# q and k of the later head pairs transposed by DMA and reordered by GpSimd, with paced loads and the mask term on ScalarE

## The chip, the cores and the metric

One core of one Trainium2 chip. The metric is the device time of one launch in microseconds (us), with smaller being better. TensorE is called PE below, VectorE DVE, ScalarE ACT, GpSimd POOL; SP is the engine that here only issues DMAs.

## The reference

Attention with four sink columns and a window of 128, then a block that mixes tokens and channels.

```python
# q, k, v: (4, 8, 768, 64); n_sink 4; window 128
scores = scale * q @ k.T
keep = (column < n_sink) | ((row - column >= 0) & (row - column < window))
a = softmax(where(keep, scores, -1e9))
x = (a @ v)  ->  (4, 768, 512), heads side by side

theta = x @ w_theta
zr, zi = x * cos(theta), x * sin(theta)
u = x + w_tok_r @ zr + w_tok_i @ zi          # over tokens
out = u + maximum(u @ w_ch, 0)
```

## The kernel before

The 32 heads are worked in 16 **pairs**, pair i in **slot** i. Slots 4 to 7 belong to batch entry 1, 8 to 11 to entry 2, 12 to 15 to entry 3; behind each four there is a theta stage (`thp`, cosine and sine `cs`, products `zz`). While a slot computes scores, PE fills its gaps with the token mixing (`yp`) and channel mixing (`wp`) of the batch entry before. PE, ACT, POOL and SP take instructions in program order. DVE's order is fixed when the kernel is built, by a scheduler that works with modelled times.

q and k must be transposed. Pairs 0 to 11 are loaded so that partition p holds rows 6p to 6p+5 (long runs in memory), cast to bf16 by POOL, transposed by PE, and put into row order by the copy that evacuates PSUM. Pairs 12 to 15 are loaded in short runs so that the DMA transpose gives the right order at once:

```python
QK_DMA = range(12, NPAIR)

def transposed_by_dma(i):                # called in slot i - 2
    if i not in QK_DMA: return
    for name in ("q", "k"):
        c = qk_c.pop((name, i))
        x = qkt.tile([P, S], BF16, name=f"{name}T", tag=f"{name}T")
        nc.sync.dma_start_transpose(out=x..., in_=c...)
        qk_t[name, i] = x

def transposed(name, i):                 # called in slot i - 1
    if i in QK_DMA: return
    for t in range(NT):                  # 6 blocks of 128 x 128
        nc.tensor.transpose(out=tp[:, t, :], in_=c[:, t, :, :], identity=ident)
    dst, src = x.rearrange("c (p t) -> c p t", t=NT), tp.rearrange("c t p -> c p t")
    ...                                  # nc.scalar.copy, or DVE for pairs 1 to 3
```

In the second half of the mixing the transposes of `u` for token blocks 0 to 2 of entries 1 and 2 go by DMA too, and so do three of four transposes of x (`xT`):

```python
U_PE = {(b, t) for b in range(B) for t in range(NT) if b in (0, B - 1) or t in (3, 4, 5)}
```

The values of the sink columns for entries 2 and 3 are copied from a f32 tile to bf16, times a row mask, four copies each (`vsink<-vsf,rows`). In program order they follow slots 8 and 9:

```python
def sink_values(b):
    for tb in range(NB):
        nc.vector.tensor_scalar(out=vsinks[b % 2][:, tb, :, 0:D], in0=vsf[:, b - 2, :, :],
                                scalar1=rows[:, tb:tb + 1], scalar2=None, op0=ALU.mult)
```

The softmax here doesn't subtract the row's maximum and nothing guards it: scores larger than these inputs give would overflow.

## Time and profile before

| | kernel before |
|---|---|
| time, three runs | 191.49 us (191.43 to 191.65) |
| span in the profile | 189.7 us |
| granted PE clock, mean | 0.998 |
| PE busy | 171.6 us, 90% |
| DVE, ACT, POOL busy | 127.4, 99.6, 70.3 us |

PE is the bound from about 90 us on. To read the timelines: the first two numbers are the start and the length of an instruction (or of x instructions in a row) in us; then the engine, the line of the kernel, the operation, what it writes and reads, the shapes; in brackets the idle time of the engine just before, and what ended it. The theta stage of entry 1 on DVE:

```profile
80.72 1.29 DVE L319 TENSOR_TENSOR zz<-cs,x_nat 128x1024 bf16<-128x1024 bf16 x2 [3.99 <-ACT cs L316]
81.93 0.48 DVE L421 TENSOR_SCALAR vsink<-vsf,rows 128x512 bf16<-128x512 f32 x1
82.64 1.29 DVE L319 TENSOR_TENSOR zz<-cs,x_nat 128x1024 bf16<-128x1024 bf16 x2 [0.23 <-ACT cs L316]
```

Two products take 1.29 us (0.65 each), DVE had been idle for 3.99 before them, and one of the eight sink copies slips in between. Seven come behind. Line numbers are higher in the kernel after: L319 here is L326 there, L421 is L429.

### The profile page before, as it was taken

What the parts mean: (1) busy time and instruction counts of PE and PEld (TensorE: products, weight loads), DVE (VectorE), ACT (ScalarE), POOL (GpSimd) and SP (SyncE); (2) the same over time, 40 slices, a digit from 0 to 9 for tenths busy, and PEclk for the clock granted to TensorE, in tenths of its full rate; (3) what the DMA queues carried; (4) which work ended last, traced back from release to release, by engine and by line L of the source; (5) the groups of instructions that cost most, each with busy time, mean ns of one, the idle gap of its engine ahead of it and who ended that gap; (6) DMA issues with size and microseconds to landing.
All of it is one profiled execution on the core that took longest, in us unless ns stands there. A gap on an engine that the chain in (4) does not pass through costs nothing.

```text
span 189.7 us, 4058 instructions
## 1 busy us (share of the span) xinstructions
PE 171.6 (90%) x1632; PEld 87.8 (46%) x1659; DVE 127.4 (67%) x237; ACT 99.6 (53%) x106; POOL 70.3 (37%) x87
## 2 busy tenths in 40 slices
PE   7776998899998998997999999999999999899972
PEld 2333574554464655443454555434345643344430
DVE  6597676883857788189969673787769726644541
ACT  4575787616973661899965702797462059000000
POOL 8986577858886601314635001670000000000000
PEclk9999999999999999999999999999999999999999
DMA  5999999999999995991239779999623500021121
GB/s 181 318 273 214 321 380 328 371 329 322 340 358 323 299 261 148 236 218 31 83 66 167 167 130 228 217 218 146 153 45 97 152 21 38 30 80 55 59 110 56
DMA packets 65954, 35.88 MB, mean 189 GB/s; under 512 B 54160, under 2 KB 60304, under 8 KB 65936
## 3 DMA queue, kind: packets, MB, share of 16 engines
q1 hardware_dynamic: 64784, 35.59, 74.6%
q0 software_dynamic: 1152, 0.04, 0.6%
q8 instruction: 13, 0.21, 0.5%
q14 instruction: 5, 0.04, 0.1%
HBM read 25.82 MB, written 6.29 MB: 169 GB/s over the span
## 4 chain that ended last, share of the span: by engine, by line
PE 59%; DVE 17%; ACT 14%; DMA 4%; issue 3%; SPq 1%; ACTq 1%
PE yp L348 24%; PE wp L376 9%; PE thp L306 8%; PE sc L207 5%; PE avp L253 5%; ACT E L220 4%; DMA kf<-in_k_dram 4%; ACT cs L315 4%; DVE E L223 4%; ACT cs L316 3%; PE tp L181 3%; DVE zz L319 3%; PE utp L367 2%; DVE x_nat L259 2%; PE xtp L283 1%
## 5 line engine op out<-in xcount | busy, mean ns | idle before, releaser
L220 ACT ACTIVATE E<-sc 128x1024 bf16<-128x1024 f32 x48 | 48.4, 1027 | 23.7 <-PE sc L207 17.6
L348 PE MATMUL yp<-zz,wrT 128*128 128x512 bf16 x141 | 53.5, 380 | 1.0 <-DVE zz L319 0.2
L348 PE MATMUL yp<-zz,wiT 128*128 128x512 bf16 x134 | 50.9, 380 | 0.8 <-DVE wiT L337 0.4
L223 DVE TENSOR_TENSOR E<-E,mask 128x2048 bf16<-128x2048 bf16 (+1 forms) x26 | 26.4, 1029 | 12.2 <-ACT E L220 12.1
L74 POOL TENSOR_SCALAR q<-qf 128x768 bf16<-128x768 f32 x14 | 14.4, 1031 | 44.0 <-PE tp L181 23.4
L319 DVE TENSOR_TENSOR zz<-cs,x_nat 128x1024 bf16<-128x1024 bf16 x24 | 19.4, 844 | 10.3 <-ACT cs L316 10.2
L376 PE MATMUL wp<-wch,uT 128*128 128x512 bf16 x86 | 23.5, 380 | 2.5 <-DVE uT L369 1.9
L379 DVE SCALAR_TENSOR_TENSOR of<-wp,u 128x512 f32<-128x512 f32 x24 | 16.4, 685 | 13.7 <-PE wp L376 13.1
L306 PE MATMUL thp<-wth,xT 128*128 128x512 bf16 x95 | 22.6, 379 | 0.4 <-ACT cs L316 0.4
L348 PEld LDWEIGHTS <-wiT 128*128 128x128 bf16 x144 | 14.0, 98 | 14.9 <-issue 2.4
L207 PE MATMUL sc<-qT,kT 64*128 64x256 bf16 x192 | 18.0, 265 | 2.7 <-DVE kT L187 2.2
L315 ACT ACTIVATE cs<-thp,half_pi 128x1024 bf16<-128x1024 f32 (+1 forms) x13 | 13.6, 1050 | 12.6 <-PE thp L306 12.4
L348 PEld LDWEIGHTS <-wrT 128*128 128x128 bf16 x144 | 14.1, 98 | 11.8 <-issue 1.5
L74 POOL TENSOR_SCALAR vx<-vf 128x768 bf16<-128x768 f32 x16 | 17.8, 1117 | 3.8 <-DMA vf<-in_v_dram 3.8
L253 PEld LDWEIGHTS <-E 128*128 128x128 bf16 x480 | 17.1, 97 | 3.8 <-issue 0.7
L352 DVE TENSOR_TENSOR u<-yp,x_nat 128x512 bf16<-128x512 f32 x24 | 16.5, 688 | 2.9 <-PE yp L348 2.6
L74 POOL TENSOR_SCALAR k<-kf 128x768 bf16<-128x768 f32 x14 | 14.5, 1035 | 6.2 <-DMA kf<-in_k_dram 2.9
L207 PEld LDWEIGHTS <-kT 64*128 64x128 bf16 x192 | 5.6, 94 | 19.1 <-issue 14.1
L259 DVE TENSOR_TENSOR x_nat<-avp,rec 128x384 bf16<-128x384 f32 x27 | 14.2, 554 | 0.3
L306 PEld LDWEIGHTS <-xT 128*128 128x128 bf16 x96 | 9.2, 98 | 11.1 <-issue 0.9
L253 PE MATMUL avp<-vx,E 128*128 128x65 bf16 x297 | 13.2, 193 | 0.0
L376 PEld LDWEIGHTS <-uT 128*128 128x128 bf16 x96 | 7.8, 97 | 11.6 <-DVE uT L369 5.4
(68 smaller groups left out, 189.2 us busy)
## 6 DMA issues: line engine op xcount, KB each, us to landing
qf<-in_q_dram SPq DMA_DIRECT2D x16, 384.0 KB, 6.3
kf<-in_k_dram SPq DMA_DIRECT2D x16, 384.0 KB, 6.4
vf<-in_v_dram SPq DMA_DIRECT2D x16, 384.0 KB, 7.4
out_dram<-of SPq DMA_DIRECT2D x24, 256.0 KB, 2.3
wf<-in_moe_w_tok_r_dram SPq DMA_DIRECT2D x6, 384.0 KB, 6.1
wf<-in_moe_w_tok_i_dram SPq DMA_DIRECT2D x6, 384.0 KB, 7.3
sqf<-in_moe_w_theta_dram SPq DMA_DIRECT2D x2, 512.0 KB
sqf<-in_moe_w_ch_dram SPq DMA_DIRECT2D x2, 512.0 KB, 7.2
```

The source lines that it names most:

```text
L74: nc.gpsimd.tensor_scalar(out=out, in0=in_, scalar1=1.0, scalar2=1.0, op0=ALU.mult, op1=ALU.mult)
L207: nc.tensor.matmul(sc[:, e, 256 * part:256 * part + n], lhsT=kT[r, m * P:(m + 1) * P], rhs=qT[r, m * P:m * P + n], start=not biased, stop= ...
L220: nc.scalar.activation(out=E[:, :, 512 * c:512 * (c + 1)], in_=sc, func=AF.Exp, scale=SCALE)
L223: nc.vector.tensor_tensor(out=E[:, :, r], in0=E[:, :, r], in1=mask2[:, :, r], op=ALU.mult)
L253: nc.tensor.matmul(avp[:, t, :], lhsT=lhsT, rhs=rhs, start=(j == 0), stop=(j == len(seq) - 1), skip_group_check=True)
L259: nc.vector.tensor_tensor(out=x_t[b][:, hp, :, D * e:D * (e + 1)], in0=avp[:, :, 0:D], in1=rec.to_broadcast([P, NT, D]), op=ALU.mult)
L306: nc.tensor.matmul(th_t[b, g][:, st, :], lhsT=xT[:, cb, 2 * g + st, :], rhs=wth[:, cb, :], start=(cb == 0), stop=(cb == NC - 1))
L315: nc.scalar.activation(out=cs[:, part, 0, :], in_=thp[:, part, :], func=AF.Sin, bias=half_pi)
L319: nc.vector.tensor_tensor(out=z_t[b][:, 2 * g + st, :, :].rearrange("p o (c n) -> p o c n", c=HP), in0=cs[:, st, :, :].rearrange("p o (c n ...
L348: nc.tensor.matmul(yp, lhsT=wT[i][:, t, sc, :], rhs=z_t[b][:, sc, i, :], start=(j == 0), stop=(j == 2 * NT - 1))
L352: nc.vector.tensor_tensor(out=u.rearrange("p (c n) -> p c n", c=HP), in0=yp.rearrange("p (c n) -> p c n", c=HP), in1=x_t[b][:, :, t, :], o ...
L376: nc.tensor.matmul(wp, lhsT=uT[:, cb, :], rhs=wch[:, cb, :], start=(cb == 0), stop=(cb == NC - 1))
```

## The change

Its intent: take q's and k's transposes of pairs 9, 10 and 11 off PE, without the short runs in memory that the DMA path of pairs 12 to 15 needs. From pair 9 on, the loads have long runs, the DMA transposes into a raw tile, and POOL copies that tile into row order (below: the raw path, and its copies the reorderings). The loads, which had been issued in bursts, are paced at one pair a slot, four pairs ahead. At the start, the mask term (`bias`) is computed by ACT and used for all first pairs but three groups, and constants not needed yet are set later.

```diff
-    vstage = pool("vstage", 6)
+    vstage = pool("vstage", 4)
+    qkr = pool("qkr", 2)
-    BIASED = {(i, c) for i in (1, 2, 3) for c in range(3)}
-    QK_DMA = range(12, NPAIR)
+    BIASED = {(i, c) for i in range(HP) for c in range(3)} - {(0,2),(1,2),(2,2)}
+    QK_DMA = ()
+    QK_RAW = range(2 * HP + 1, NPAIR)
...
-    later = collections.deque([("w", 0), ("w", 1), ("qk", HP), ... up to pair 11])
+    later = collections.deque(["w0", "w1", "q4 v4", "w2", "q5 v5", "w3", "q6 v6", "q7", "w4 v7"])
...
     def transposed_by_dma(i):
+        if i in QK_RAW:
+            for name in ("q", "k"):
+                raw = qkr.tile([P, NT, P], BF16, name=f"{name}r", tag=f"{name}r")
+                nc.sync.dma_start_transpose(out=raw, in_=qk_c.pop((name, i))...)
+                qk_r[name, i] = raw
...
     def transposed(name, i):
+        if i in QK_RAW:
+            tp = qk_r.pop((name, i))
...
+        if i in QK_RAW:
+            pool_copy(dst, src)
...
-        nc.vector.tensor_scalar(out=bias, in0=mask, scalar1=30000.0, scalar2=-30000.0, ...)
+        nc.scalar.activation(out=bias, in_=mask, func=AF.Identity, scale=30000.0, bias=low)
...
     def slot(i, blk, wtok=None):          # cast_wtok moves to the head of the slot
...
+        if i == HP:
+            load_wtok(5)
+        if not last:
+            ahead(i)
         if hp > 0:
             weigh(i - 1, 0)
...
+    def ahead(i):
+        if i + 4 < NPAIR:
+            load_qk(i + 4)
+            load_v(i + 4)
...
-    warm(W[2])                            # 4 matmuls without use, at the start
+    later_constants()                     # vsf and rows set here, after pair 2
...
-        if b < 3:                         # two pairs at once in the theta stage
-            for n in range(2):
-                load_qk(HP * 3 + 2 * (b - 1) + n)
-                load_v(HP * 3 + 2 * (b - 1) + n)
+        ahead(i)
```

More of the change, by code (lines that the diff above doesn't have):

```diff
@@ L79 @@
     DVE_EVAC = {(name, i) for name in "qk" for i in (1, 2, 3)}
-    BIASED = {(i, c) for i in (1, 2, 3) for c in range(3)}
-    QK_DMA = range(12, NPAIR)
+    BIASED = {(i, c) for i in range(HP) for c in range(3)} - {(0,2),(1,2),(2,2)}
+    QK_DMA = ()
+    QK_RAW = range(2 * HP + 1, NPAIR)
     X_DMA = (0, 1, 2)
     U_PE = {(b, t) for b in range(B) for t in range(NT) if b in (0, B - 1) or t in (3, 4, 5)}
-    later = collections.deque([("w", 0), ("w", 1), ("qk", HP), ("v", HP), ("w", 2), ("qk", HP + 1), ("v", HP + 1),
-                               ("qk", HP + 2), ("w", 3), ("v", HP + 2), ("qk", HP + 3), ("w", 4), ("v", HP + 3),
-                               ("qk", 2 * HP), ("w", 5), ("v", 2 * HP)]
-                              + [(kind, i) for i in range(2 * HP + 1, 3 * HP) for kind in ("qk", "v")])
+    later = collections.deque(["w0", "w1", "q4 v4", "w2", "q5 v5", "w3", "q6 v6", "q7", "w4 v7"])
     def next_load():
-        if later:
-            kind, n = later.popleft()
-            (load_qk if kind == "qk" else load_wtok)(n)
-        while later and later[0][0] == "v":
-            load_v(later.popleft()[1])
+        for what in later.popleft().split() if later else ():
+            {"w": load_wtok, "q": load_qk, "v": load_v}[what[0]](int(what[1:]))
     qk_f, qk_c, qk_t, v_f, v_x, e_t = {}, {}, {}, {}, {}, {}
-    w_raw, x_t, xT_t, z_t, y_t, u_t, uT_t, th_t = {}, {}, {}, {}, {}, {}, {}, {}
+    w_raw, x_t, xT_t, z_t, y_t, u_t, uT_t, th_t, qk_r = {}, {}, {}, {}, {}, {}, {}, {}, {}
     def load_qk(i):
@@ L165, in transposed_by_dma @@
     def transposed_by_dma(i):
+        if i in QK_RAW:
+            for name in ("q", "k"):
+                raw = qkr.tile([P, NT, P], BF16, name=f"{name}r", tag=f"{name}r")
+                nc.sync.dma_start_transpose(out=raw, in_=qk_c.pop((name, i)).rearrange("p t h d -> p (t h d)"))
+                qk_r[name, i] = raw
         if i not in QK_DMA:
@@ L177, in transposed @@
             return
-        c = qk_c.pop((name, i))
-        tp = ps_sm.tile([P, NT, P], BF16, name="tp", tag="sm")
-        for t in range(NT):
-            nc.tensor.transpose(out=tp[:, t, :], in_=c[:, t, :, :], identity=ident)
+        if i in QK_RAW:
+            tp = qk_r.pop((name, i))
+        else:
+            c = qk_c.pop((name, i))
+            tp = ps_sm.tile([P, NT, P], BF16, name="tp", tag="sm")
+            for t in range(NT):
+                nc.tensor.transpose(out=tp[:, t, :], in_=c[:, t, :, :], identity=ident)
         x = qkt.tile([P, S], BF16, name=f"{name}T", tag=f"{name}T")
         dst, src = x.rearrange("c (p t) -> c p t", t=NT), tp.rearrange("c t p -> c p t")
-        if (name, i) not in DVE_EVAC:
+        if i in QK_RAW:
+            pool_copy(dst, src)
+        elif (name, i) not in DVE_EVAC:
             nc.scalar.copy(out=dst, in_=src)
@@ L386 @@
     half_pi = consts.tile([P, 1], FP32)
+    low = consts.tile([P, 1], FP32)
     NE = 11 * P
@@ L428, in constants, with later_constants @@
         nc.vector.memset(half_pi, math.pi / 2.0)
+        nc.vector.memset(low, -30000.0)
+    def later_constants():
+        nc.vector.memset(vsf, 0.0)
         nc.vector.memset(rows, 0.0)
@@ L447, in make_mask @@
         nc.gpsimd.memset(mask[0:NS, 0:2 * P], 1.0)
-        nc.vector.tensor_scalar(out=bias, in0=mask, scalar1=30000.0, scalar2=-30000.0,
-                                op0=ALU.mult, op1=ALU.add)
+        nc.scalar.activation(out=bias, in_=mask, func=AF.Identity, scale=30000.0, bias=low)
     W = [8, 1, 4, 1, 0, 3, 3]
@@ L480, in slot @@
         first, last = hp == 0, hp == HP - 1
+        if wtok is not None:
+            cast_wtok(wtok)
         if i + 2 < HP or HP <= i < NPAIR - 2:
@@ L498, in slot @@
                 next_heads(i, "q")
-        if wtok is not None:
-            cast_wtok(wtok)
         transposed_by_dma(i + 2)
@@ L544 @@
     load_sinks(1)
-    nc.vector.memset(vsf, 0.0)
     warm(W[0])
```

## The prediction

> **What bounds the kernel now.** I read the page first (share of each engine), then the stretches of 10 us, then the chain of waits and the timeline of each engine around the places that the change touches. The work falls into stages: pairs 0 to 3 with the loads (0 to 45 us), four slots with the token weights (to 76), a theta stage (to 85), slots 8 to 11 (to 113), another theta stage, slots 12 to 15, a third, and the last mixing (163 to the end).
>
> ```profile
> PE 171.6 (90%) x1632; PEld 87.8 (46%) x1659; DVE 127.4 (67%) x237; ACT 99.6 (53%) x106; POOL 70.3 (37%) x87
> ```
> ```profile
> 10.00:20.00 10.00, 7.68 (x113) 4.04 (x112) 9.03 (x12) 6.66 (x7) 6.67 (x8) 1.00 1.19 227
> ...
> 100.00:110.00 10.00, 9.89 (x123) 5.26 (x125) 8.44 (x16) 5.92 (x6) 2.25 (x2) 1.00 0.82 159
> ...
> 130.00:140.00 10.00, 9.89 (x122) 4.86 (x122) 7.30 (x15) 4.78 (x5) 0.00 (x0) 1.00 0.54 127
> ```
> The columns are busy time of PE, PEld, DVE, ACT, POOL, the clock, the DMA share and GB/s. From 90 us on TensorE is filled (9.89 of 10), so there a PE instruction that goes away is time gained, and anything else is gained only if PE waits for it. At 10 to 20 us PE waits, with VectorE at 9.03 and the DMA engines full.
>
> **Start.** Pair 0's mask product sits on VectorE between the evacuations of pair 1 and those of pair 2, and PE waits for the latter:
> ```profile
> 11.76 2.98 DVE L223 TENSOR_TENSOR E<-E,mask 128x2048 bf16<-128x2048 bf16 x2
> 14.66 0.94 DVE L187 COPY qT<-tp 128x768 bf16<-128x768 bf16 x1
> 15.53 0.94 DVE L187 COPY kT<-tp 128x768 bf16<-128x768 bf16 x1
> ```
> ```profile
> 16.53 0.39 PE L207 MATMUL sc<-qT,kT 64*128 64x256 bf16 x4 [1.29 <-DVE kT L187]
> 16.85 0.51 PE L181 MATMUL tp<-ident,q 128*128 128x128 bf16 x6
> 17.20 0.29 PE L253 MATMUL avp<-vsink,E 128*128 128x65 bf16 x4
> ```
> But the third of these needs the values of pair 0 in bf16, and they come late, by the load:
> ```profile
> 16.13 0.83 POOL L74 TENSOR_SCALAR vx<-vf 128x768 bf16<-128x768 f32 x1 [0.70 <-DMA vf<-in_v_dram]
> ```
> They are ready at 16.13 + 0.83 = 16.96. PE takes instructions in program order, so it cannot pass that place before 16.96, whatever VectorE does: 17.20 - 16.96 = 0.24 us is all that the place itself can give.
>
> **Slots.** The first exp of slots 9, 10, 11 and of 13, 14, 15 gives their pitch:
> ```profile
> 97.05 1.02 ACT L220 ACTIVATE E<-sc 128x1024 bf16<-128x1024 f32 x1 [1.81 <-PE sc L207]
> ...
> 103.51 2.10 ACT L220 ACTIVATE E<-sc 128x1024 bf16<-128x1024 f32 x2 [1.81 <-PE sc L207]
> ...
> 134.39 2.10 ACT L220 ACTIVATE E<-sc 128x1024 bf16<-128x1024 f32 x2 [1.82 <-PE sc L207]
> ...
> 140.18 2.10 ACT L220 ACTIVATE E<-sc 128x1024 bf16<-128x1024 f32 x2 [1.81 <-PE sc L207]
> ```
> 103.51 - 97.05 = 6.46 us where PE transposes q and k of the next pair, 140.18 - 134.39 = 5.79 where the DMA already does: 0.67 for 12 transposes, 56 ns each. (The 220 ns of the groups is latency; the starts of two neighbouring groups of six lie 0.33 to 0.34 apart.)
>
> **What the skill says.** "VectorE: DVE Perf Modes", The three transpose paths, gives 390 ns for a 128x128 transpose on TensorE and 1309 ns through the DMA; this trace has 56 ns as the cost per transpose in the stream, and 4.1 us from issue to landing for a whole q (six blocks). So the DMA path has long latency but costs PE nothing. "SBUF — State Buffer", Who interferes with whom: a VectorE instruction with two SBUF inputs contends with a GpSimd one that reads SBUF, and the second to start waits for the whole of the first. The trace agrees: the mask product of 2048 columns takes 1.23 us at 105.65 with GpSimd idle and 1.67 at 99.89 beside casts, where two casts of values took 1.80 each instead of 0.83. "ScalarE: Activation LUTs", What ACT_TABLE_LOAD costs, puts an ACTIVATE with a pointer bias at 280 ns + 0.833 ns per element: 1.45 us for the 1408 columns of the mask term, an estimate from that page; the trace's own such instruction, the 1024-column cosine, takes 1.11 (280 + 853 = 1.13), so it agrees. VectorE does it in 0.53.
>
> **The change, part by part.**
>
> (a) Pairs 9, 10, 11: 3 x 12 = 36 transposes leave PE, and 6 copies of 0.80 leave ScalarE. Pairs 12 to 15 had none to lose. Slots 9 and 10 (which prepare 10 and 11) are PE-filled: -0.67 each, -1.34. Slot 8 ends differently, on a wait:
> ```profile
> 85.98 2.80 DVE L421 TENSOR_SCALAR vsink<-vsf,rows 128x512 bf16<-128x512 f32 x4
> 88.71 0.41 DVE L369 COPY uT<-utp 128x512 bf16<-128x512 bf16 x1
> ```
> ```profile
> 89.18 1.04 PE L376 MATMUL wp<-wch,uT 128*128 128x512 bf16 x4 [0.84 <-DVE uT L369]
> ```
> There PE already waits 0.84, so removing 12 transposes alone would only lengthen the wait. But those four VectorE copies took 0.70 each, as GpSimd cast pair 11 at 83.76 to 87.7: that cast waited for the cast buffer of pair 9, held until PE's transposes at 83.1 to 85.5. Now the DMA frees it in slot 7, so I expect the cast to move ahead of 84 us, the four copies to fall to about 0.45 each (one alone takes 0.48), and uT to come about 1.0 earlier. PE, 0.67 ahead, then waits some 0.5. I count -1.0 for slot 8. Sum of (a): -2.3.
>
> (b) In exchange GpSimd gets 14 copies of 128x768 bf16 (pairs 9 to 15). I take 0.9 each, as the cast of as many elements takes 0.83 to 1.1: 12.6 us, so POOL goes from 70 to some 83 us. Per slot it then has two casts of q and k, one of v and two reorderings, 5 x 0.9 to 1.1 = 4.5 to 5.5 us of a 5.8 us slot: it fits. Latency fits too: issued in slot i, the transpose lands 4 us later, is reordered in slot i+1, and is read in slot i+2. What it costs is VectorE: per slot a 2048 and a 768 product meet it, (1.67 - 1.23) + (1.04 - 0.55) = 0.9 at worst, on top of about 5.0 busy: full, in the slots where it all falls together. Nearly all of it is slack by a slot; I charge +0.3 for slots 9 to 14.
>
> (c) Start. Pair 0 takes its mask from PE in two of three groups: the 2048 product goes, two 768 products (pairs 1 and 2) come, the mask term (0.53) moves to ScalarE, where it falls between the cast of q and its evacuation (5.04, when the mask is done, to about 6.5); the evacuations follow at 6.5 and 7.3, so the first exp stays near 8.5. Pair 1 comes 0.44 earlier (its evacuations follow the cast directly), pair 2's kT falls from 16.4 to about 14.5, and PE then stands at the values until 16.96. Behind that: the third group of pair 2 loses its bias matmuls (0.49), and the evacuation of k for pair 3 meets a free VectorE. Walking the program from 16.96 with an exp each 1.0 us, the last exp of pair 3 ends at 24.0 instead of 24.9: I take -0.85. The theta sums after it need the second half of w_theta, cast by 25.0, before their first use at 28, so they follow. PE's bias columns rise by 8960 - 8448 = 512 over the four pairs, 0.2 us, in the waiting stage. The four warming matmuls that go (7.1 to 8.1) give way to bias matmuls in the same gap.
>
> (d) Loads paced: last use of a late load was GpSimd's wait of 15.2 us before the q cast at 117, which held up nobody. Pairs 12 to 15 come in runs of 1536 bytes instead of 256. PE waits for no load after 30 us, so 0. Token weights cast first in a slot: GpSimd's order only, 0 with a spread of 0.5.
>
> Sum: -2.3 + 0.3 - 0.85 + 0 = -2.85, from 191.5: **188.6 us**, 1.5% faster.
>
> **Rivals.** First, the start gives more: if the values landed earlier, or if the wait at the values were not the last, the 1.9 us that pair 2 gains would count in full, and the time would be 187.4. For it: VectorE is at 9.03 of 10 there. Against: GpSimd idles for the load before each of the four value casts and both of w_theta, with the DMA at its limit. Second, VectorE becomes the bound in slots 8 to 14: it is at 8.44 of 10 in slot 10 with 2.25 us of POOL, and POOL doubles. If each of six slots lost the 0.9, 5 us would go and it would end at 192 to 193. Against: the products' results are read a slot later. Third, the reordering is far slower than 0.9 (its reads step by 256 bytes): at 1.8 it fills GpSimd (3 + 3.6 us a slot) and scores wait for it; 191 to 194. Fourth, the constants moved behind pair 2 (memset of vsf, 0.91, and five small ones) land on VectorE just before the last division of the first stage, 26.5 us, which leads to theta: +1.0, that is 189.6. VectorE's order is chosen by a scheduler (the change of order of lines L404 to L431 shows it), so this is open.
>
> **Range and chances.** The sure part is 1.3; slot 8 (0 to 1), start (-0.3 to 2.0) and contention (0 to 2) spread it. Range **186.8 to 190.7**. Faster by over 2% needs less than 187.7: 0.26. Slower by over 2%: 0.04. Within: 0.70.
>
> **What would show it.** Right: slots 8 to 10 at 5.8 us pitch with no transposes of q and k after pair 8; 14 POOL copies near 0.9; the first av matmul still just after the first value cast, near 17.0; mask term on ACT 1.4; theta's first cosine near 28.8 instead of 29.65; slots 12 to 15 unchanged within 0.3. Wrong: reordering above 1.5 us, PE waiting on qT or kT of POOL, pitches over 6.0, value casts well ahead of 16 us, or an added table load for the mask term.

## The result, and the profile after

| | before | after |
|---|---|---|
| time, median of four runs | 191.57 us (191.43 to 192.12) | 205.93 us (205.18 to 208.03) |
| span in the profile | 189.7 us | 204.6 us |
| granted PE clock, mean | 0.998 | 0.971 |

The kernel after is **slower by 7.6%** (ratio 1.0761, 95% interval 1.0678 to 1.0845); the result is correct. Ratios here and below are the recorded ones, of one kernel's fast runs to the other's fast runs of the same rounds, so they are not quite the ratio of the medians quoted, nor always that of the plain means (e6 below: 1.0032 recorded, 1.0002 from the means of its three fast runs and of all runs of before). The time of before differs between the rounds (medians 190.96 to 191.75), so experiments are compared by their ratios; a percentage point is 1.915 us.

The page of the kernel after, its first line, and the group of q's reorderings from the groups by line (the columns are busy us, mean ns of one, idle time before them):

```profile
PE 174.3 (85%) x1592; PEld 86.6 (42%) x1619; DVE 134.7 (66%) x238; ACT 96.8 (47%) x101; POOL 88.8 (43%) x101
...
L75 POOL TENSOR_SCALAR qT<-qr 128x768 bf16<-128x768 bf16 x7 | 12.2, 1737 | 14.3 <-DMA qr<-q 14.3
```

PE does 40 instructions fewer than before, as planned (36 transposes and 4 warming matmuls), and is still busy longer. DVE is busy 7.3 us longer with one instruction more. A reordering takes 1.74 us on average.

**Where the time went** can be dated by when the same instruction comes in both traces (us, from the timelines):

| first instruction of | before | after | difference |
|---|---|---|---|
| first cosine, entry 0 | 29.65 | 28.95 | -0.7 |
| evacuation of q, pair 8 | 74.79 | 74.51 | -0.3 |
| scores of slot 9 | 90.1 | 95.6 | +5.5 |
| scores of slot 11 | 103.1 | 108.4 | +5.3 |
| theta sums, entry 2 | 115.2 | 125.6 | +10.3 |
| scores of slot 13 | 128.2 | 142.6 | +14.4 |
| end | 189.7 | 204.6 | +14.9 |

So there are three jumps, of 4 to 6 us each: the theta stage of entry 1, slots 10 and 11, and the theta stage of entry 2. The stretches of 10 us (busy PE, PEld, DVE, ACT, POOL with instruction counts, clock, DMA share, GB/s) show the same:

```profile
80.00:90.00 10.00, 5.18 (x19) 1.63 (x17) 10.00 (x11) 3.85 (x5) 7.83 (x6) 0.84 0.08 17
...
110.00:120.00 10.00, 6.78 (x64) 3.52 (x64) 4.67 (x9) 1.95 (x2) 4.96 (x6) 0.88 0.92 202
```

In the first, DVE is busy without a break with only 11 instructions, while PE has 5 us of work. In the second DVE, ACT and POOL are half idle and only the DMA engines are full (0.92). These are two different troubles. PE's timeline, its long waits alone:

```profile
86.53 0.38 PE L355 MATMUL yp<-zz,wrT 128*128 128x512 bf16 x1 [3.53 <-DVE zz L326]
...
88.43 0.58 PE L355 MATMUL yp<-zz,wrT 128*128 128x512 bf16 x1 [1.10 <-DVE zz L326]
...
108.39 0.39 PE L214 MATMUL sc<-qT,kT 64*128 64x256 bf16 x4 [1.13 <-POOL kT L75]
...
116.56 1.04 PE L383 MATMUL wp<-wch,uT 128*128 128x512 bf16 x3 [3.17 <-DMA uT<-u]
...
128.02 1.47 PE L313 MATMUL thp<-wth,xT 128*128 128x512 bf16 x6 [1.88 <-DMA xT<-x_nat]
...
139.40 0.38 PE L355 MATMUL yp<-zz,wrT 128*128 128x512 bf16 x1 [1.31 <-DVE zz L326]
```

Before, the longest wait of PE between 70 and 160 us was the 0.84 at 89.18 that the prediction shows. Now they are 3.53, 1.10, 1.13, 3.17, 1.88 and 1.31: 12.1 us of waits, of three kinds (DVE's products, POOL's reordering, DMA transposes). The rest of the loss lies in shorter waits and in PE's longer busy time, and is not divided here.

**First kind.** DVE's timeline, and POOL's over the same time:

```profile
76.37 8.24 DVE L429 TENSOR_SCALAR vsink<-vsf,rows 128x512 bf16<-128x512 f32 x7
84.53 3.85 DVE L326 TENSOR_TENSOR zz<-cs,x_nat 128x1024 bf16<-128x1024 bf16 x2
```
```profile
78.10 1.68 POOL L75 TENSOR_SCALAR qT<-qr 128x768 bf16<-128x768 bf16 x1
79.75 1.68 POOL L75 TENSOR_SCALAR kT<-kr 128x768 bf16<-128x768 bf16 x1
...
84.29 1.64 POOL L75 TENSOR_SCALAR qT<-qr 128x768 bf16<-128x768 bf16 x1
85.91 1.92 POOL L75 TENSOR_SCALAR kT<-kr 128x768 bf16<-128x768 bf16 x1
100.20 0.83 POOL L75 TENSOR_SCALAR q<-qf 128x768 bf16<-128x768 f32 x1 [12.38 <-DMA qf<-in_q_dram]
```

Seven sink copies now come **ahead** of the first product and take 8.24 us, 1.18 each where one alone took 0.48; the two products behind them take 3.85, or 1.92 each where they took 0.65. All of it happens while POOL runs nine instructions back to back (76.34 to 87.83, casts and reorderings), some of them work for slots 8 and 9, ahead of PE. The products begin to be available at 86.5 instead of about 81.4. The last line is the other trouble: POOL then stands for 12.38 us, waiting for the load of pair 12.

**Second kind.** SP's timeline of before, then of after, around slots 8 to 10:

```profile
90.14 1.30 SPq L358 DMA_TRANSPOSE uT<-u  x1
...
95.72 1.20 SPq L358 DMA_TRANSPOSE uT<-u  x1
...
102.57 1.22 SPq L358 DMA_TRANSPOSE uT<-u  x1
```
```profile
78.59 1.24 SPq L166 DMA_TRANSPOSE kr<-k  x1
95.00 1.65 SPq L365 DMA_TRANSPOSE uT<-u  x1
96.71 0.57 SPq L111 DMA_DIRECT2D qf<-in_q_dram  x1
...
100.64 1.26 SPq L166 DMA_TRANSPOSE qr<-q  x1
...
103.32 1.22 SPq L365 DMA_TRANSPOSE uT<-u  x1
...
106.36 4.30 SPq L304 DMA_TRANSPOSE xT<-x_nat  x1
...
114.07 1.23 SPq L365 DMA_TRANSPOSE uT<-u  x1
```

SP issues nothing between 78.59 + 1.24 and 95.00: the next in its order is the transpose of u, which DVE has not made yet, and the load of pair 12 stands behind it. When u comes, everything is due at once, and from 95 to 127 us SP issues without a break. The transposes of u, one a slot (5.6 to 6.9 us apart before), are now 8.3 and 10.75 us apart. The one that PE needs at 116.56 goes out at 114.07. POOL's kT of pair 11, which PE needs at 108.39, begins with a transpose that goes out only at 100.64. DVE's timeline, of before and then of after, shows when the third u is made:

```profile
101.48 0.68 DVE L352 TENSOR_TENSOR u<-yp,x_nat 128x512 bf16<-128x512 f32 x1
...
105.51 0.69 DVE L359 TENSOR_TENSOR u<-yp,x_nat 128x512 bf16<-128x512 f32 x1 [0.32 <-PE yp L355]
```

Before, its transpose goes out 0.41 us after u is ready (102.16); after, 7.87 us after (106.20), and PE has it 2.49 us later. The median from issue to landing of these transposes is 2.5 us, where it was 3.0 before. So this wait is made in SP's order and not by a slower transfer. More than half of the 7.87 is the issue of one transpose of x, 4.30 us right behind three loads; with no loads between, the two at 97.50 and 103.88 of the kernel before took 1.22 and 1.24.

### The profile page after: what moved, and what is told of

Read it like the earlier page. It is cut to its first block, busy times and chain, and to the rows that moved or that the text cites. A ratio compares the mean times of both kernels' runs of the same rounds, so it can differ in the third digit from the quotient of the medians.

```text
span 204.6 us, 4001 instructions
## 1 busy us (share of the span) xinstructions
PE 174.3 (85%) x1592; PEld 86.6 (42%) x1619; DVE 134.7 (66%) x238; ACT 96.8 (47%) x101; POOL 88.8 (43%) x101
## 4 chain that ended last, share of the span: by engine, by line
PE 46%; DVE 22%; DMA 12%; ACT 10%; issue 4%; SPq 2%; POOL 2%; ACTq 0%; DVEq 0%; POOLq 0%
PE yp L355 20%; PE wp L383 7%; DVE zz L326 6%; PE thp L313 5%; DMA vf<-in_v_dram 5%; DVE E L230 4%; DVE vsink L429 4%; PE sc L214 4%; ACT E L227 3%; PE avp L260 3%; DMA xT<-x_nat 2%; DVE u L359 2%; SPq L111 2%; ACT cs L323 2%; DMA qr<-q 2%
## 5 line engine op out<-in xcount | busy, mean ns | idle before, releaser
L227 ACT ACTIVATE E<-sc 128x1024 bf16<-128x1024 f32 x48 | 48.6, 1026 | 28.8 <-PE sc L214 20.3
L355 PE MATMUL yp<-zz,wrT 128*128 128x512 bf16 x141 | 55.0, 390 | 7.6 <-DVE zz L326 6.6
L355 PE MATMUL yp<-zz,wiT 128*128 128x512 bf16 x133 | 52.2, 393 | 0.9 <-DVE wiT L344 0.4
L230 DVE TENSOR_TENSOR E<-E,mask 128x768 bf16<-128x768 bf16 (+1 forms) x27 | 26.1, 977 | 14.4 <-ACT E L227 14.4
L326 DVE TENSOR_TENSOR zz<-cs,x_nat 128x1024 bf16<-128x1024 bf16 x24 | 22.8, 989 | 6.2 <-ACT cs L323 6.2
L75 POOL TENSOR_SCALAR q<-qf 128x768 bf16<-128x768 f32 x14 | 12.1, 862 | 32.9 <-DMA qf<-in_q_dram 22.2
L75 POOL TENSOR_SCALAR qT<-qr 128x768 bf16<-128x768 bf16 x7 | 12.2, 1737 | 14.3 <-DMA qr<-q 14.3
L75 POOL TENSOR_SCALAR vx<-vf 128x768 bf16<-128x768 f32 x16 | 17.2, 1077 | 2.0 <-DMA vf<-in_v_dram 1.9
L376 DVE COPY uT<-utp 128x512 bf16<-128x512 bf16 x18 | 7.6, 420 | 10.8 <-PE utp L374 10.7
```

The lines of the kernel that those rows point to most:

```text
L75: nc.gpsimd.tensor_scalar(out=out, in0=in_, scalar1=1.0, scalar2=1.0, op0=ALU.mult, op1=ALU.mult)
L227: nc.scalar.activation(out=E[:, :, 512 * c:512 * (c + 1)], in_=sc, func=AF.Exp, scale=SCALE)
L230: nc.vector.tensor_tensor(out=E[:, :, r], in0=E[:, :, r], in1=mask2[:, :, r], op=ALU.mult)
L326: nc.vector.tensor_tensor(out=z_t[b][:, 2 * g + st, :, :].rearrange("p o (c n) -> p o c n", c=HP), in0=cs[:, st, :, :].rearrange("p o (c n ...
L355: nc.tensor.matmul(yp, lhsT=wT[i][:, t, sc, :], rhs=z_t[b][:, sc, i, :], start=(j == 0), stop=(j == 2 * NT - 1))
```

## The experiments

"After with X undone" is the kernel after with an edit, the others start from the kernel before. All results are correct except e3's. Runs over 1.5% above the fastest of the same kernel count as slow and are left out of the ratios (two of e4's four, one each of e6, e9, e10 and e13). Two parts of the change are in no run alone: the casts of the token weights at the head of the slot, and the four buffers for v instead of six.

### e1: reordering on ScalarE

```diff
-            pool_copy(dst, src)
+            nc.scalar.copy(out=dst, in_=src)
```

> The changed kernel, with the 14 reordering copies on ScalarE instead of GpSimd; the loads, the DMA transposes and the order of VectorE stay (seven of the eight sink copies still stand ahead of the first zz product of the theta stage at 76 us). Theory A (GpSimd's added copies hold VectorE[...]: 8.24 us for seven sink copies, 3.85 for two zz, 4.53 for four zz later) expects the sink copies under 5 us, zz near 0.65 to 0.9 each, and 190 to 196 us in all. Theory B (the SP queue: paced loads and transposes issued one behind the other, so that pair 12 is loaded and pair 11 reordered late) expects 200 us or more, with the late load of pair 12 still there.

Measured: 199.76 us (198.44 to 200.76), ratio 1.0458 [1.0396, 1.0520]: 3.0 points better than after. DVE's timeline of it:

```profile
76.12 5.73 DVE L429 TENSOR_SCALAR vsink<-vsf,rows 128x512 bf16<-128x512 f32 x7
81.77 1.28 DVE L326 TENSOR_TENSOR zz<-cs,x_nat 128x1024 bf16<-128x1024 bf16 x2
```

The products are back at 0.64 each, and the sink copies fall from 1.18 to 0.82 each. So POOL's reorderings lengthen DVE's work. Moving them is worth some 6 us, which counts PE's wait for POOL's kT too (1.13 in the kernel after, gone here) and is net of what they cost on ACT. But 4.6% stay: the waits for uT (2.10) and xT (1.21) are still there, if shorter, and ACT now makes PE wait 1.36 and 0.83.

### e2: no raw path, pacing and start kept

```diff
-    QK_DMA = ()
+    QK_DMA = range(12, NPAIR)
-    QK_RAW = range(2 * HP + 1, NPAIR)
+    QK_RAW = ()
```

> The changed kernel without its new transposing path: pairs 9 to 11 on TensorE and 12 to 15 straight by DMA, as before; the paced loads, the mask term on ScalarE and the later constants stay, and so do the hoisted sink copies. Theory A expects 189 to 192 us (the start gives 0.7, the rest as before). Theory B, if the pacing of the loads is enough by itself, expects 196 us or more; if pacing and the extra transposes together are needed, as A.

Measured: 195.64 us (194.59 to 196.84), ratio 1.0248 [1.0189, 1.0308]. Without a single reordering and with the old transposes, the paced loads still lose 2.5% (by the 2% rule the verdict is unclear, as the interval reaches below 1.02). PE's waits:

```profile
109.19 0.81 PE L383 MATMUL wp<-wch,uT 128*128 128x512 bf16 x3 [0.81 <-DMA uT<-u]
119.39 2.04 PE L313 MATMUL thp<-wth,xT 128*128 128x512 bf16 x6 [2.50 <-DMA xT<-x_nat]
```

Besides 1.02 us for x, which DVE makes, it is DMA transposes that PE waits for; no product. So the pacing is a cause of its own. The seven sink copies come ahead of the products here too, but take 4.03 us with no reordering beside them, and hold up nobody.

### e3: after without the sink copies (wrong)

```diff
                 if b == 2 and hp < 2:
-                    sink_values(2 + hp)
+                    pass
```

> The changed kernel without the eight sink copies (wrong result on purpose for batches 2 and 3, nothing waits for them otherwise). If the order of VectorE, sink copies ahead of zz, is what costs the first 6 us, the time falls by 5 to 8 to 198 to 201. If GpSimd's copies would then hit zz instead, by 2 to 4 only, to 202 to 204. Theory B alone: no change beyond 1.5 us.

Measured: 200.71 us (199.76 to 201.63), ratio 1.0506 [1.0441, 1.0570]. Taking the copies away gives back 2.6 points, not all: the products still meet POOL (four in 4.69 us, two in 3.28), and PE still waits 3.37 for uT.

### e4: before with the raw path alone

```diff
-    vstage = pool("vstage", 6)
+    vstage = pool("vstage", 4)
+    qkr = pool("qkr", 2)
-    QK_DMA = range(12, NPAIR)
+    QK_DMA = ()
+    QK_RAW = range(2 * HP + 1, NPAIR)
     # and the edits of transposed_by_dma and transposed, as in the change
```

> The kernel before with nothing but the new transposing path for pairs 9 to 15 (DMA into a raw tile, reordered by GpSimd; 4 buffers for v instead of 6 to make room). Loads and start as before; VectorE has only one sink copy between the first zz pairs, as before. Theory A (GpSimd contention by itself) expects 195 to 201 us, with zz of 1 us and more in the two theta stages. Theory B (loads paced through the SP queue) expects 188 to 191.

Measured: 198.42 us over all four (195.75 to 199.39, two of them slow), ratio of the two fast ones 1.0314 [1.0221, 1.0408]. The raw path loses 3% by itself. PE's waits are for products (1.06 and 0.56, later 1.31, 0.31 and 0.64) and for a copy of DVE (2.10) that stands behind two sink copies of 3.37 together; none of 0.3 or more is for a DMA transpose. So the two troubles come apart: e4 has the first, e2 the second.

### e5 and e6: after with the old loads; and with both undone

e5 puts back the list `later` of the kernel before and its loads in the theta stage, and drops `ahead`. e6 is e5 with the edit of e1.

```diff
     # and the old list of loads
...
-        if i == HP:
-            load_wtok(5)
-        if not last:
-            ahead(i)
...
-        ahead(i)
+        if b < 3:
+            for n in range(2):
+                load_qk(HP * 3 + 2 * (b - 1) + n)
+                load_v(HP * 3 + 2 * (b - 1) + n)
```

> The changed kernel with the loads as before: the old list of loads and the four pairs of loads ahead of the theta stages, none inside the slots of batch 2 (the order of VectorE follows: four zz ahead of the sink copies). Pacing theory: the run without the raw path lost some 5 us to paced loads, so this gains at least that, 197 to 200 us, and the waits for the DMA of uT and xT and for kT of GpSimd go. Contention theory alone: within 1.5 us of the changed kernel, except for what the order of the sink copies gives (up to 5).

> The changed kernel with both suspects undone: loads as before and the 14 reordering copies on ScalarE. If the two causes account for the loss, 189 to 192 us, near the kernel before; if a third is at work (the extra DMA transposes, the buffers, the longer way of q and k), 194 or more.

Measured: e5 196.45 us (195.53 to 197.43), ratio 1.0266 [1.0207, 1.0324]; e6 192.00 us (190.33 to 194.81), ratio 1.0032 [0.9956, 1.0109]. In e5 PE waits for no DMA transpose any more, only for products and once for x (0.56):

```profile
88.30 0.59 PE L361 MATMUL yp<-zz,wrT 128*128 128x512 bf16 x1 [3.05 <-DVE zz L332]
```

The four kernels make a square (excess over before):

| | paced loads | old loads |
|---|---|---|
| reordering on GpSimd | +7.6% (after) | +2.7% (e5) |
| reordering on ScalarE | +4.6% (e1) | +0.3% (e6) |

The pacing costs 4.9 points (9.5 us) in one row and 4.3 (8.2 us) in the other; GpSimd instead of ScalarE costs 3.0 points (5.8 us) and 2.3 (4.5 us). With both undone, no loss is left that is clear of noise. The square also bears on the casts of the token weights: e5 is e4 with these casts and the new start, and e4's 1.0314 less the 0.4 points that e8 below gives for the start is 1.027, e5's own ratio. So they cost nothing that these runs show.

### e7: the lower clock

PE's clock was 0.82 to 0.88 behind the long waits. e7 adds 16 matmuls without use behind the theta stage of entry 1, before slot 8's mixing has its products, so that PE does not stand idle there.

```diff
+        if b == 1:
+            warm(16)
```

> The changed kernel with 16 dummy matmuls (3.5 us) where TensorE stood 3.5 us for zz before slot 8. The wait for zz stays, only its filling changes. If the lower granted clock after the wait (0.84 and 0.82 in the two stretches from 80 to 100 us) is a cost of its own, the clock there rises to about 0.95 or more and the time falls by 1.5 to 3.5. If the clock only falls while nothing waits for it, no change within 1.

Measured: 205.50 us (205.01 to 207.87), ratio 1.0762 [1.0685, 1.0840]: no change. The stretches of it:

```profile
84.00:88.00 4.00, 3.35 (x15) 1.36 (x14) 4.00 (x3) 0.00 (x0) 4.00 (x3) 1.00 0.00 0
88.00:96.00 8.00, 6.76 (x42) 2.16 (x41) 6.14 (x10) 6.27 (x6) 0.16 (x1) 0.79 0.01 2
```

The clock is full where the extra matmuls run, and the low stretch came a little later all the same. So the experiment did not remove the lower clock, and what it costs by itself stays open.

### e8: before with the start changes alone

Mask term by ACT, the new set `BIASED`, `later_constants`, no `warm(W[2])`, everything else as before.

```diff
-    BIASED = {(i, c) for i in (1, 2, 3) for c in range(3)}
+    BIASED = {(i, c) for i in range(HP) for c in range(3)} - {(0,2),(1,2),(2,2)}
-        nc.vector.tensor_scalar(out=bias, in0=mask, scalar1=30000.0, scalar2=-30000.0, ...)
+        nc.scalar.activation(out=bias, in_=mask, func=AF.Identity, scale=30000.0, bias=low)
...
-    warm(W[2])
+    later_constants()
```

> The kernel before with the changes of the start alone: mask term on ScalarE, pair 0 masked by TensorE in two groups, constants moved behind pair 2, four warming matmuls less. Prediction's step (c): the first cosine at 28.8 to 29.0 instead of 29.65 and 190.0 to 191.2 us (0.3 to 1.2 less than before), and the values of pair 0 still the wait. If the gain at the start is lost again later: no difference.

Measured: 190.76 us (189.54 to 191.24), ratio 0.9958 [0.9899, 1.0016]: -0.8 us, with an interval that just includes no gain at all. In its profile, of the fastest of the four runs (189.54), the first cosine comes at 27.92, earlier than the 28.8 to 29.0 expected.

### e9: the paced loads ahead of the slot's transposes

The loads move from near the slot's end to its head, so that the load of pair 12 does not stand behind the transpose of u.

```diff
         if i + 1 < HP or HP <= i < NPAIR - 1:
             cast_v(i + 1)
+        if i == HP:
+            load_wtok(5)
+        if not last:
+            ahead(i)
```

> The changed kernel with each slot's loads (two slots ahead, as they are) put at the slot's head in the SP queue, ahead of the transposes of q, k, u and x, instead of behind those of q, k and u. The order of VectorE with its hoisted sink copies is the same. If the pacing costs by position (the load of pair 12 stood behind a transpose of u that was not ready from 80 to 95 us, and what follows stood behind the loads), the load of pair 12 goes out near 82 us and the time falls by 3 to 6, to 200 to 203. If it costs by place in time (any load inside slots 8 to 11 delays the transposes behind it), no gain: 204 to 208.

Measured: 205.33 us (203.07 to 206.54), ratio 1.0709 [1.0641, 1.0777]. The load goes out at 74.08 instead of 96.71, and nothing clear of noise is gained. PE waits 2.24 and 1.30 for products beside the reorderings (the kernel after: 3.53 and 1.10), and now 1.85 more for one beside POOL's casts of pair 12. It also waits 3.53 for uT: that u is ready at 105.48, and its transpose goes out at 113.73, behind the next pair's loads and transposes. Bringing that load forward by itself does not help.

### e10: the source of the sink copies loaded later

```diff
-                if hp == 1:
+                if hp == 3:
                     load_later_sinks()
```

In the kernel after this load was issued at 60.20 us, before at 63.87, since fewer loads stand ahead of it. The idea is that the scheduler that fixes DVE's order thus had the copies ready ahead of the products. e10 tests the link. The load goes behind slot 7.

> The changed kernel with one move: the small loads of the sink rows are issued after slot 7 instead of slot 5, so that the scheduler puts all eight sink copies behind the six zz products instead of seven of them ahead. If the hoisted order is a cause of its own, the first zz of that stage no longer waits 8.2 us, and the time falls by 3 to 6, to 200 to 203, with the slots of batch 2 still losing 5 by the SP queue. If GpSimd's copies then take the zz products instead, the gain is under 2.

Measured: 201.26 us (199.09 to 203.26), ratio 1.0498 [1.0431, 1.0564]: 2.6 points, 5.0 us, better than after, as much as without the copies at all (e3). DVE's timeline:

```profile
79.38 4.59 DVE L326 TENSOR_TENSOR zz<-cs,x_nat 128x1024 bf16<-128x1024 bf16 x4 [4.01 <-ACT cs L323]
```

The products are first again, but four take 4.59 us (1.15 each), as they still meet POOL. Of the kernels with the sink load after slot 5, those with the paced loads whose timelines I read (after, e1, e2, e9) all have seven copies first, and those with the old loads (before, e4, e5, e6) do not. The order on DVE is therefore part of the price of the pacing.

### e11 and e12: what is left of the transposes' gain

e11 is e8 with the edit of e10. e12 is e11 with pairs 9 to 11 transposed by DMA in the old way, with short runs and without reordering.

```diff
-    QK_DMA = range(12, NPAIR)
+    QK_DMA = range(2 * HP + 1, NPAIR)
```

> Toward a better version: the kernel before with the start alone changed, and the sink rows loaded after slot 7. The wait of TensorE for uT behind the sink copies (0.84 before, 0.90 in the start-only run) should go or shrink: 189.8 to 190.8 us, 0.4 to 0.9% faster than before. If the sink copies then hold the mask products of slot 8 or 9, no better than the start alone (190.8).

> As the run before, and pairs 9 to 11 transposed by DMA straight into place as pairs 12 to 15 always were (loads in 256-byte runs, no raw tile, nothing for GpSimd). The prediction's step (a) without its price: slots 8 to 10 lose 12 transposes each, 0.67 us: 188 to 189 us, 1.2 to 1.8% faster. If the SP queue, with 2.5 us of transposes more in three slots, delays uT or xT, 190 to 194.

Measured: e11 190.81 us (189.81 to 191.68), ratio 0.9983 [0.9943, 1.0024]; e12 189.70 us (189.40 to 190.87), ratio 0.9948 [0.9906, 0.9990]. Loading the sinks later gains nothing where POOL is not in the way. The 36 transposes give 0.35 points, 0.7 us, of the 2.3 predicted, and the intervals overlap: in e12 PE waits 1.11 us for u at 94.5, which DVE makes behind late sink copies.

### e13: loads of pairs 12 to 15 issued by ScalarE

```diff
     def ahead(i):
         if i + 4 < NPAIR:
-            load_qk(i + 4)
-            load_v(i + 4)
+            by = nc.scalar if i >= 2 * HP else None
+            load_qk(i + 4, by)
+            load_v(i + 4, by)
```

> The changed kernel with the loads of pairs 12 to 15 issued from ScalarE's queue at the same places, so that the SP queue has nothing but transposes and stores in slots 8 to 11. If the SP queue itself is the bound there (it issues without a gap from 95 to 127 us, 10.7 us for the round of slot 10), the waits of TensorE for the DMA of uT (3.2) and xT (1.9) and for GpSimd's kT (1.1) go and the time falls by 4 to 7, to 199 to 202. If the DMA engines are the bound (loads and transposes share them whoever issues), the waits stay and the time is within 1.5 of 205.9.

Measured: 207.26 us (205.85 to 211.21), ratio 1.0791 [1.0741, 1.0842]: no gain. The only profile fell on the slow run (211.21), so its waits for uT (4.06 and 3.60) are not compared in size. So taking the loads out of SP's order does not help. But in that profile ACT's own order held the loads too, so this does not settle how much is the share of the DMA engines and how much is order. A hint: SP's transposes of q, k and u from 106.08 took 3.36, 2.35 and 2.83 us to issue there, though SP issues no load between them.

### e14: u transposed by PE in entry 1

```diff
-    U_PE = {(b, t) ... if b in (0, B - 1) or t in (3, 4, 5)}
+    U_PE = {(b, t) ... if b in (0, 1, B - 1) or t in (3, 4, 5)}
```

> The changed kernel with the three transposes of u in slots 8 to 10 on TensorE (4 x 56 ns each) instead of by DMA. The SP queue loses 3 x 1.22 us of issue and nothing waits on a DMA for uT: if the wait for uT (3.2) is the chain's own, the time falls by 2 to 4, to 202 to 204; if the wait for xT or for kT of GpSimd just takes its place, by under 1.5.

Measured: 200.93 us (200.78 to 201.21), ratio 1.0491 [1.0448, 1.0534]: 2.7 points, 5.2 us, better than after, though PE gets 12 transposes more. On SP, the load of pair 12 follows the transposes of q and k directly:

```profile
78.80 0.57 SPq L111 DMA_DIRECT2D qf<-in_q_dram  x1
```

PE's waits for uT and xT are gone, without a load or a reordering being moved; those for products (3.52, 0.88, 1.18) stay. So the transposes of u in SP's order, beside loads, were the links by which the second trouble reached PE. Note that e9 also brought the load of pair 12 forward and gained nothing: the early load by itself is not what helps; what e14 adds is that the transpose of u is gone.

### e15: a version without the troubles

The start changes of e8, pairs 9 to 11 by the old DMA path of e12, the old loads, and the sink copies on ACT, after slots 7 and 11.

```diff
-            nc.vector.tensor_scalar(out=vsinks[b % 2][:, tb, :, 0:D], in0=vsf[:, b - 2, :, :],
-                                    scalar1=rows[:, tb:tb + 1], scalar2=None, op0=ALU.mult)
+            nc.scalar.activation(out=vsinks[b % 2][:, tb, :, 0:D], in_=vsf[:, b - 2, :, :],
+                                 func=AF.Copy, scale=rows[:, tb:tb + 1])
...
-                if b == 2 and hp < 2:
-                    sink_values(2 + hp)
+                if b == 2 and hp == 3:
+                    sink_values(3)
...
+                if hp == 3:
+                    sink_values(2)
```

> A version meant to beat both: the kernel before with the changed start, pairs 9 to 11 transposed by DMA straight into place, and the eight sink copies on ScalarE in places where it idles (behind slot 7 and behind slot 11) instead of on VectorE. Expected from the run without that last step (189.7, where TensorE still waited 1.11 for u behind sink copies): 188.0 to 189.2 us, 1.0 to 1.7% faster than before. If the copies delay the exp or cosine behind them: 189.5 to 191.

Measured: 188.98 us (188.09 to 190.06), ratio **0.9871** [0.9833, 0.9910], correct: 1.3% faster than before, with an interval that excludes no gain. The page of it:

```profile
PE 169.1 (91%) x1592; PEld 85.5 (46%) x1619; DVE 122.2 (66%) x230; ACT 101.4 (54%) x109; POOL 67.2 (36%) x87
```

DVE is down 5.2 us from before and POOL 3.1, PE has the same 1592 instructions as the kernel after and does them in 169.1 us, and no wait of PE between 70 and 180 us is over 0.65.

## Why the prediction was wrong

It said 188.6 us, and 205.93 came. The steps in order:

**(c) Start: right in size, in part by luck.** Predicted -0.85 with the first cosine near 28.8. It came at 28.95 (before: 29.65), and e8 measured -0.8 us for the start changes alone. The mask term took 1.47 us on ACT, where 1.45 was estimated, and it brought no table load. PE did come to wait for the values of pair 0 (0.73, until 16.95). But the 16.96 that PE "cannot pass" is no fixed bound: POOL's first cast of values waits for the load in every profile, and the first product with them (`avp<-vx`) starts at 15.26 to 17.21 in the fifteen profiles with the new start, and the first cosine at 27.27 to 29.22; in the two with the old start (before, e4) they come at 17.32 and 17.52, and at 29.65 and 29.85. So the first rival, that the start gives more, came true in part of the profiles. The prediction also misread a line: the `avp<-vsink` at 17.20 does not need these values (in the kernel after it starts at 15.93); `avp<-vx` behind it, at 17.32, does.

**(a) Transposes, -2.3: part right.** Slots 9 to 10 came to a pitch of 5.80 (95.60 to 101.40), so the 0.67 of that slot was there. The sub-step for slot 8 (-1.0) failed: it held that POOL's cast of pair 11 would move ahead and that DVE's sink copies would get faster. The cast did move (to 81.40), but two pairs of reorderings came into the same stretch, and seven copies at 1.18 us stood ahead of the products. Measured without the raw path, with DMA transposes straight into place, the gain was 0.7 us (e12 against e11), and at most 1.7 us when the sink copies also leave DVE (e15 against e8).

**(b) Reordering, +0.3: the first term mis-sized.** Two assumptions in it failed. A reordering was taken at 0.9 us, from the cast of as many elements; it took 1.48 at its shortest (114.07) and 1.74 on average for q. And contention was charged to mask products, whose results are needed a slot later. It fell on the sink copies (0.48 to 1.18) and the products zz (0.65 to 1.92), which PE waits for at once. Measured: 4.5 us (e5 against e6) to 5.8 us (after against e1). The prediction's second and third rivals named both mechanisms, but placed them in the slots and not in the theta stage, and set their ends at 191 to 194. Of the signs that it named for being wrong, three came: reorderings above 1.5 us, PE waiting on POOL's kT (1.13), and a pitch over 6.0 (slots 10 to 11, 6.99).

**(d) Pacing, 0: the second term mis-sized, and the largest.** "PE waits for no load after 30 us, so 0" was the step. It is true that PE does not wait for loads. But the loads share the DMA engines, and SP's order, with transposes that PE does wait for, and they came into slots 8 to 11 where these are made; and an earlier load of sink rows turned DVE's order round. Measured: 8.2 to 9.5 us in the square; by e10 some 5.0 of the 9.5 are DVE's order, and the rest, 4.4 (e10 against e5), is what is left of the pacing. Even without the raw path it costs 5.6 us (e2 against e8).

The terms as measured, each from two neighbouring kernels: start -0.8 (e8); raw path with reordering on ACT, transposes' gain, buffers and casts of token weights included, +1.4 (e6 over e8, not clear of noise); reordering on GpSimd instead +4.5 (e5 over e6, net of its cost on ACT); pacing without the turned order +4.4 (e10 over e5); the turned order +5.0 (after over e10). The sum is 14.5 us, by construction the whole loss but for rounding. Each is known to some 1 to 2 us, and they depend on each other: that e2, with the turned order but no reordering, has no wait for products shows that the order costs PE nothing there without POOL's reorderings. Two ends of the prediction's rivals don't follow from its own terms: the first comes to 187.6 and not 187.4, the second to 193.4 and not 192 to 193.

**Open:** how the remaining cost of the pacing divides between the DMA engines' share and SP's order. In the kernel after, the longest wait for a DMA transpose (3.17, for uT) is made in SP's order; why a transpose there takes up to 4.30 us to issue behind loads is not shown (e9, e13 and e14 bear on it; the profile of e13 is slow). Open too is what the lower clock after waits costs (e7 only moved it).

## What to carry to other kernels

Before moving work to a queue or an engine "with room", list what stands there next to the new work and who waits for *that*: loads that nobody waits for can hold up transposes that PE needs, and a copy on GpSimd can lengthen products on VectorE. Where a scheduler fixes an engine's order, a load that is issued a few us earlier can turn that order round; compare the order of both kernels before trusting a sum of durations. Take the price of a copy from one with the same access pattern, not from one with as many elements.

## What the Trainium skill lacked or had wrong

- "SBUF — State Buffer", Who interferes with whom: the rule holds, in that products with two SBUF inputs and one-input `tensor_scalar` copies on VectorE both lengthened beside GpSimd, and moving the reordering to ScalarE took it away for the products (0.64) and in part for the copies (0.82). What it lacks is the size for chains of instructions on both engines: 0.65 became 1.92 us per product and 0.48 became 1.18 us per copy.
- "GPSIMD Engine Reference", 4.1 Engine selection, calls one-input work on GpSimd roughly line-rate. A reordering of 768 bf16 elements took 1.48 us where the f32-to-bf16 cast of 768 took 0.83, 78% more. The same page's section 7, written for kernels of one's own on the engine, gives +50% for reads with a step over 8 bytes, and here the step is 256 bytes. No run here separates the step from the input type, which is bf16 and not f32. If the step is the cause, the ordinary copy should be named there; the prediction named the step in its third rival, but its sum kept the 0.9 us of the cast.
- "DMA: Bandwidth & Descriptors": its section on the DMA transpose gives no time to issue one (a count elsewhere on the page is for another kind, out of HBM). Here the issue alone held SP for 1.20 to 1.30 us in most cases and for 4.30 us right behind three loads (106.36), while these loads took 0.46 to 0.57 each.
